# Threshold attention and two MoE layers: the last score tile of each head in one pass, its main term added inside the maximum

## The chip, the cores and the metric

One core of one Trainium2 chip. The metric is device time in microseconds (us) of one launch; lower is better. The kernel before took 969.99 us, the median of three runs (968.16 to 970.31 us).

## The reference, cut to what matters

Attention over 4 batches, 8 heads, 576 positions and 64 channels, with a threshold that is relative to each row's maximum; then two feed-forward layers over 2304 tokens. Only the attention is touched.

```python
scores = scale * np.matmul(q, k.transpose(0, 1, 3, 2))
thresh = np.max(scores, axis=-1, keepdims=True) - tau
scores = np.where(scores >= thresh, scores, -1000000000.0)
...
attn = np.exp(scores)
attn = attn / (np.sum(attn, axis=-1, keepdims=True) + 1e-09)
return np.matmul(attn, v).astype(np.float32)
```

## The kernel before, in words

**Numbers in two halves.** TensorE multiplies in a shortened fp32 (fp32r), so every operand is split into a high part and a low rest. A product is the high-by-high term (the main term) plus two cross terms. For each head, `q_st` holds q's low part on partitions 0 to 63 and its high part on 64 to 127; `k_st` holds k's high part on 0 to 63 and its low part on 64 to 127. One pass over 128 partitions therefore gives both cross terms at once. A second pass over `q_m` (q's high part on partitions 0 to 63, and rows for the shift under them) and `k_on` gives the main term.

**Attention twice over.** For each of 32 heads the kernel first computes scores with queries on partitions, only to find each query's maximum: `scores` (L319) makes five tiles of 128 queries by 576 keys, two passes of two matmuls of 288 columns each, and `row_max` (L335, its instruction L339) reduces each tile on VectorE into one column of `mcol`. 576 queries are four and a half tiles, so the fifth tile (n = 4) has 64 real queries; its other 64 stationary columns are zeros, put into `q_st[:, 576:640]` once by `setup_fill` (L181). `row_shift` (L343) turns the maxima into shifts, `shift_turn` transposes them and `shift_store` (L366) copies them with ScalarE (L369) and issues a DMA from ScalarE's own queue (L370) that puts them into `q_m`.

Then `shifted` (L390, matmuls L403) computes the scores once more with keys on partitions, less the shift, `expo` (L416) takes the exponential on ScalarE, `mask` (L421) zeroes what lies under the threshold on VectorE, `p_split` splits the result (L429 on ScalarE, L430 on GpSimd), and `values` (L435, matmuls L453) multiplies by V: three groups of two matmuls for each tile, high P by high V, high P by low V, low P by high V. `v_hi` is 128 columns wide: 64 of V, and 64 of ones, of which one gives the row sums. `v_lo` is 64 wide. `store_head` (L459) copies a finished head out of PSUM on ScalarE (`xs`, L465), and SyncE's DMA queue stores it (L467, L468).

**Order.** Heads go in pairs; a pair has nine units of work, 144 units in all, each with one tile of shifted scores. I call nine units of a pair a round. The instructions of each unit are emitted in an order written out by hand, one string for each place in the round (`ORDER`, L71): E is the shifted tile and its exponential (and, where due, the turn and store of the shifts), S a score tile, x a maximum, M the mask, v one group of value matmuls, V the rest of them, L the store of a finished head, P the transposes of a later head (L271), F its split (L279 on ScalarE, L280 on VectorE), T loads and the DMAs that stack K and Q, p the split of P. Each engine runs its own instructions in that order. The last score tile of a pair's first head falls on unit 3 of a round, that of its second head on unit 7 (15 rounds have both; the two heads of the first pair come in a ramp ahead):

```python
"FESvSSxxMxxpVLAPTJ",     # unit 3 of the round
"FEvvSvSSMxxxVLPvATpJ",   # unit 7
"FSEvPSSTMxxxpVLAJ",      # unit 8
```

**Buffers.** Scores, shifted scores and transposes share three PSUM buffers; one goes to the next tile in the order in which the tiles before were released (a score tile by its maximum, a shifted tile by its mask, a transpose by its split). The value sums have one PSUM buffer, which is free for the next head when `xs` has been copied out. In unit 7 the first head of the pair is stored; in unit 8 the value sums of the second begin.

**Stacking.** `stack_k` (L285) and `stack_q` (L293) fill the stacked operands by DMAs of the SyncE queue: `k_both` from `q_st` (L289) and from `lo` (L290), `q_m` from `q_st` (L291), and two units later `q_st` from `lo` (L295).

Of the kernel before, what the change touches and what calls it, by code (L numbers as in the profile page):

```python
# [9 lines left out]
F32 = mybir.dt.float32  # L10
# [11 lines left out]
def kernel(  # L22
# [83 lines left out]
    def f32(ap):  # L106
        return ap.bitcast(F32)
# [51 lines left out]
    q_st = bufs4([P, SP], F32R, "q_st")  # L159
    q_m = bufs4([R3, SP], F32R, "q_m")  # L160
    NV = 10
    v_nat = [early_p.tile([P, NV, D], F32, name=f"v_nat{i}") for i in range(2)]
    v_hi = [att_p.tile([P, NV, P], F32R, name=f"v_hi{i}") for i in range(2)]
    v_lo = [att_p.tile([P, NV, D], F32R, name=f"v_lo{i}") for i in range(2)]
    scale2 = const.tile([P, 1], F32, name="scale2")
    nat_both = [early_p.tile([P, 2, NM + 1, 2, D], F32, name=f"nat{i}") for i in range(2)]
# [13 lines left out]

    def setup_fill(i, eng):  # L181

        for j in range(2):
            if i < NBUF[j]:
                pad = slice(S, SP) if j == 0 else slice(0, 64)
                eng.memset(f32(k_st[j][i][:, pad]), 0.0)
                eng.memset(f32(k_on[j][i][:, pad]), 0.0)
                eng.memset(f32(k_on[j][i][D:R3, 64 * j : 64 * j + S]), 1.0)
                eng.memset(f32(k_on[j][i][D:R1, 64 * j : 64 * j + S]), 0.0)
                eng.memset(f32(q_st[j][i][:, S:SP]), 0.0)  # L190
                eng.memset(f32(q_m[j][i][0:D, S:SP]), 0.0)
                eng.memset(f32(q_m[j][i][D:R3, :]), 0.0)
# [5 lines left out]

    def setup_ones():
        for t in v_hi:  # L200
            nc.gpsimd.memset(f32(t[:, 0:8, D:P]), 1.0)
            for half in range(2):
                for n in range(2):
                    nc.gpsimd.memset(f32(t[64 * half : 64 * half + 64, 8 + n, D:P]), float(n == half))

    nat_t = {}
    k_rows, q_rows, v_rows = (a.rearrange("b h s d -> (b h s) d") for a in (k, q, v))
# [77 lines left out]
    def stack_k(h):  # L285
        j, i = buf(h)
        o = slice(key_off(h), key_off(h) + S)
        kh = f32(q_st[j][i][0:D, 0:S]).unsqueeze(1).to_broadcast([D, 2, S])
        nc.sync.dma_start(f32(k_both[j][i][0:D, :, o]), kh)  # L289
        nc.sync.dma_start(f32(k_st[j][i][D:P, o]), f32(tr_t[h][0:D, :]))  # L290
        nc.sync.dma_start(f32(q_m[j][i][0:D, 0:S]), f32(q_st[j][i][D:P, 0:S]))  # L291

    def stack_q(h):  # L293
        j, i = buf(h)
# [2 lines left out]
    def split_first():  # L297

        srcs = [tr_t[h] for h in range(2)]
        for h in range(2):  # L300
            split_kq(h)
            j, i = buf(h)
            o = slice(key_off(h), key_off(h) + S)
            nc.scalar.copy(k_st[j][i][0:D, o], f32(q_st[j][i][0:D, 0:S]))
            nc.vector.tensor_copy(k_on[j][i][0:D, o], srcs[h][0:D])
            nc.sync.dma_start(f32(k_st[j][i][D:P, o]), f32(tr_t[h][0:D, :]))
            stack_q(h)
            nc.gpsimd.tensor_copy(q_m[j][i][0:D, 0:S], f32(q_st[j][i][D:P, 0:S]))

    def keep_warm(n):  # L310

# [3 lines left out]

    sc_ps = {}
    mcol = {}

    def scores(h, n):  # L319
        j, i = buf(h)  # L320
        o = key_off(h)
        ps = ps_r.tile([P, 2, 512], F32, tag="r", name="sc")
        for st, kk in ((q_st, k_st), (q_m, k_on)):
            r = slice(0, P if st is q_st else R1)
            for c in range(2):
                nc.tensor.matmul(  # L326
                    ps[:, c, 0:HS],
                    lhsT=st[j][i][r, n * P : n * P + P],
                    rhs=kk[j][i][r, o + c * HS : o + (c + 1) * HS],
                    start=(st is q_st),  # L330
                    stop=(st is q_m),
                )
        sc_ps[h, n] = ps

    def row_max(h, n):  # L335
        if n == 0:
            mcol[h] = att_p.tile([P, NTI], F32, tag="mcol", name="mcol", bufs=2)
        mc = mcol[h]
        nc.vector.tensor_reduce(  # L339
            mc[:, n : n + 1], sc_ps.pop((h, n))[:, :, 0:HS], axis=AXES.XY, op=ALU.max, negate=True  # L340
        )
# [93 lines left out]
    def values(u, j):  # L435
# [12 lines left out]
            av_ps[h] = ps_av.tile([P, 2, 512], F32, tag="av", name="av")  # L448
        ps = av_ps[h]
        vh, vl = v_hi[p % 2][:, vn, :], v_lo[p % 2][:, vn, :]  # L450
        for o, vv, pp in ((P, vh, hi), (D, vl, hi), (P, vh, lo)):
            for c in range(2):
                nc.tensor.matmul(  # L453
                    ps[0:o, c, 0:HS], lhsT=vv, rhs=pp[:, c, :],
                    start=first and pp is hi and o == P, stop=last and pp is lo,
                )
            yield

    def store_head(h):  # L459
# [2 lines left out]
            xs = att_p.tile([P, 2, HS], F32, tag="xs", name="xs", bufs=2)  # L462
        else:
            xs = raw_p.tile([P, 1024], F32, tag="raw", name="xs")[:, 0:S].rearrange("p (c s) -> p c s", c=2)
        nc.scalar.copy(xs, av_ps.pop(h)[:, :, 0:HS])  # L465
        r = slice(D * (hh % 2), D * (hh % 2) + D)
        nc.sync.dma_start(sums_d[b][hh : hh + 1, :], xs[D : D + 1].rearrange("p c s -> p (c s)"))  # L467
        nc.sync.dma_start(x[r, hh // 2, b * S : (b + 1) * S], xs[0:D].rearrange("p c s -> p (c s)"))  # L468
# [250 lines left out]
    def attention_unit(u):  # L719
# [6 lines left out]
        av = itertools.chain(*av)  # L726
        sc = iter(s_at.get(u, ()))
        mx = iter(s_at.get(u, ()))
        for what in ORDER[u % UNITS]:
            if what == "E" and 0 <= u < NU:  # L730
                shifted(u)
# [7 lines left out]
                    scores(*a)  # L739
            elif what == "x":  # L740
                for _, a in itertools.islice(mx, 1):
                    row_max(*a)
            elif what == "M" and 0 <= u < NU:
                mask(u)
            elif what == "p" and 0 <= u - 1 < NU:
                p_split(u - 1)
            elif what == "V":
# [423 lines left out]
```

## Time and profile before

| what | value |
|---|---|
| median of three runs | 969.99 us |
| the profiled execution | 968.04 us, of which the span from first to last instruction 966.3 us |
| granted TensorE clock, mean | 0.999 |
| TensorE matmul busy | 944.8 us (98%), 5299 matmuls |
| VectorE, ScalarE, GpSimd busy | 711.9, 493.9, 603.3 us |
| attention | about the first 365 us; the two layers follow |

Busy time of TensorE is modelled, since matmuls overlap: what tells its pace is the distance from one start to the next. PEld is the weight load that goes ahead of each matmul. In a timeline row the first number is the start, the second the time taken, x2 says that two instructions are merged, and the bracket is the idle time before with what ended it.

### The profile page before, as it was taken

How to read it: one execution, taken by the hardware profiler on the slowest of the kernel's cores; microseconds unless marked ns; L12 is line 12 of the kernel's file. 1: busy time of each engine (PE TensorE's matmuls, PEld its weight loads, DVE VectorE, ACT ScalarE, POOL GpSimd, SP SyncE). 2: the span in 40 equal slices, each digit the busy share in tenths (PEclk: the TensorE clock that was granted, in tenths of full speed). 3: DMA queues.
4: the chain of work that ended last, by engine and by line, in shares of the span. 5: the costliest groups of instructions: out<-in, count | busy, mean ns of one | idle time of the engine just before them, and what ended most of it. 6: DMA issues, size and time to landing. Idle time of an engine off the chain costs nothing.

```text
span 966.3 us, 15184 instructions
## 1 busy us (share of the span) xinstructions
PE 944.8 (98%) x5299; PEld 842.3 (87%) x5299; DVE 711.9 (74%) x1132; ACT 493.9 (51%) x924; POOL 603.3 (62%) x575
## 2 busy tenths in 40 slices
PE   7999999999999989999999999999999999999998
PEld 7899899999989978889888988898889988888886
DVE  5788888788788875898678876888675676666562
ACT  3667677777767675354333433333334444344433
POOL 7678788888978898677445544654547614334422
PEclk9999999999999999999999999999999999999999
DMA  6665666657666314211311131112311124444443
GB/s 144 148 147 124 152 159 145 170 126 176 157 142 154 81 44 98 68 66 44 120 44 66 44 119 45 65 45 77 129 34 45 44 66 131 109 120 124 138 119 90
DMA packets 89726, 99.61 MB, mean 103 GB/s; under 512 B 50000, under 2 KB 62608, under 8 KB 89648
## 3 DMA queue, kind: packets, MB, share of 16 engines
q1 hardware_dynamic: 87952, 97.97, 38.5%
q8 instruction: 42, 0.69, 0.3%
q10 hardware_dynamic: 1696, 0.66, 0.3%
q14 instruction: 36, 0.29, 0.1%
HBM read 55.13 MB, written 15.88 MB: 73 GB/s over the span
## 4 chain that ended last, share of the span: by engine, by line
PE 79%; POOL 8%; issue 4%; DVE 4%; ACT 3%; DMA 1%; ACTq 0%; POOLq 0%; DVEq 0%
PE y L833 18%; PE h L793 18%; PE o L988 10%; PE h L877 10%; PE av L453 9%; PE zt L403 6%; PE sc L326 6%; POOL plo L430 3%; PE tr L271 1%; POOL wg L560 1%; DMA nat<-in_q_dram 1%; DVE mcol L339 1%; POOL dec_a L531 1%; POOL xl L769 1%; ACT phi L429 1%
## 5 line engine op out<-in xcount | busy, mean ns | idle before, releaser
L430 POOL TENSOR_TENSOR plo<-e,phi 128x576 fp32r<-128x576 f32 x144 | 207.6, 1451 | 48.9 <-ACT phi L429 48.8
L816 POOL TENSOR_TENSOR gl<-cl,gh 128x512 fp32r<-128x512 f32 (+1 forms) x80 | 100.3, 1254 | 160.0 <-ACT gh L815 85.3
L793 PE MATMUL h<-xh,wg 128*128 128x512 f32 (+1 forms) x640 | 184.1, 369 | 0.7 <-DVE e L421 0.7
L833 PE MATMUL y<-gh,wg 128*128 128x512 f32 (+1 forms) x640 | 184.6, 369 | 0.0
L421 DVE SCALAR_TENSOR_TENSOR e<-zt,ntau,e 128x576 f32<-128x576 f32 x144 | 117.3, 815 | 54.5 <-ACT e L416 34.8
L793 PEld LDWEIGHTS h<-xh,wg 128*128 128x128 f32 x640 | 118.4, 188 | 16.7 <-DVE e L421 1.0
L833 PEld LDWEIGHTS y<-gh,wg 128*128 128x128 f32 x640 | 118.5, 188 | 15.9
L416 ACT ACTIVATE e<-zt 128x576 f32<-128x576 f32 x144 | 93.9, 652 | 70.0 <-PE zt L403 53.2
L339 DVE TENSOR_REDUCE mcol<-sc 128x1 f32<-128x576 f32 x160 | 116.7, 748 | 4.9 <-PE sc L326 4.7
L833 PE MATMUL y<-gl,wg 128*128 128x512 f32 (+1 forms) x320 | 118.8, 371 | 0.9 <-POOL gl L816 0.9
L793 PE MATMUL h<-xl,wg 128*128 128x512 f32 (+1 forms) x320 | 117.8, 368 | 0.0
L815 ACT CAST gh<-cl 128x512 fp32r<-128x512 f32 (+1 forms) x80 | 46.3, 579 | 111.9 <-DVE cl L814 110.7
L812 ACT ACTIVATE cl<-cl,half 128x512 f32<-128x512 f32 (+1 forms) x80 | 54.4, 679 | 95.4 <-DVE cl L811 95.4
L988 PE MATMUL o<-wg,ln 128*128 128x512 f32 x432 | 102.7, 393 | 0.0
L877 PE MATMUL h<-wg,y 128*128 128x512 f32 x432 | 101.1, 390 | 0.0
L988 PEld LDWEIGHTS o<-wg,ln 128*128 128x128 f32 x432 | 80.9, 188 | 18.8 <-ACT ln L951 0.4
L429 ACT CAST phi<-e 128x576 fp32r<-128x576 f32 x144 | 96.2, 668 | 1.5 <-ACT mt L369 0.7
L952 POOL TENSOR_TENSOR ln<-land,ln 128x1024 fp32r<-128x1024 f32 x16 | 38.5, 2404 | 91.7 <-ACT ln L951 85.0
L877 PEld LDWEIGHTS h<-wg,y 128*128 128x128 f32 x432 | 81.0, 188 | 16.8
L811 DVE TENSOR_SCALAR cl<-h 128x512 f32<-128x512 f32 (+1 forms) x80 | 50.6, 632 | 51.1 <-PE h L793 49.0
L326 PE MATMUL sc<-k_both,q_st 128*128 128x288 f32 x320 | 72.2, 307 | 6.5 <-issue 1.8
L403 PE MATMUL zt<-q_st,k_both 128*128 128x288 f32 x320 | 72.4, 308 | 1.6 <-DVE lo L280 1.3
(114 smaller groups left out, 1883.2 us busy)
## 6 DMA issues: line engine op xcount, KB each, us to landing
raw<-in_moe_w_in_dram SPq DMA_DIRECT2D x24, 512.0 KB
raw<-in_moe_w_out_dram SPq DMA_DIRECT2D x24, 512.0 KB
k_both<-q_st SPq DMA_DIRECT2D x30, 288.0 KB
sq<-so SPq DMA_DIRECT2D x64, 128.0 KB
land<-sq SPq DMA_DIRECT2D x16, 512.0 KB
k_both<-lo SPq DMA_DIRECT2D x32, 144.0 KB
q_st<-lo SPq DMA_DIRECT2D x32, 144.0 KB
x<-xs SPq DMA_DIRECT2D x32, 144.0 KB
```

Source lines behind the costliest of these rows:

```text
L326: nc.tensor.matmul(ps[:, c, 0:HS], lhsT=st[j][i][r, n * P : n * P + P], rhs=kk[j][i][r, o + c * HS : o + (c + 1) * HS], start=(st is q_st) ...
L339: nc.vector.tensor_reduce(mc[:, n : n + 1], sc_ps.pop((h, n))[:, :, 0:HS], axis=AXES.XY, op=ALU.max, negate=True)
L403: nc.tensor.matmul(ps[:, c, 0:HS], lhsT=st, rhs=mv[:, c * HS : (c + 1) * HS], start=(m == 0), stop=(m == len(todo) - 1),)
L416: nc.scalar.activation(out=e, in_=st_ps[u][:, :, 0:HS], func=ACTF.Exp)
L421: nc.vector.scalar_tensor_tensor(out=e, in0=st_ps.pop(u)[:, :, 0:HS], scalar=ntau[:, 0:1], in1=e, op0=ALU.is_ge, op1=ALU.mult)
L429: nc.scalar.copy(hi, e)
L430: (nc.vector if u - NU in LO_DVE or u < NU - UNITS and u % UNITS in LO_UNITS else nc.gpsimd).tensor_tensor(lo, e, f32(hi), op=ALU.subtract)
L793: nc.tensor.matmul(ps, lhsT=a[:, kk, f], rhs=m[:, kk, :], start=(n == 0 and kk == 0), stop=(n == 2 and kk == KD - 1),)
L816: nc.gpsimd.tensor_tensor(gl, cl, f32(gh), op=ALU.subtract)
L833: nc.tensor.matmul(y_ps[c][d], lhsT=a[:, jj, ds_], rhs=m, start=(jj == 0 and n == 0), stop=(jj == JG - 1 and n == 2),)
L877: nc.tensor.matmul(ps[g], lhsT=a[:, kk, :], rhs=wg_t["in2", g][s][:, kk, :], start=(n < 2), stop=(n >= 6 * KD - 2),)
L988: nc.tensor.matmul(ps, lhsT=a[:, f, :], rhs=wg_t["out2", f // 4][m][:, f % 4, :], start=(n == 0), stop=(n == len(terms) - 1))
```

## The change

In `scores`, the fifth tile does only the first pass. For that, the zero columns of `q_st` (partitions 0 to 63) get q's high part of the last 64 queries, by one more DMA in `stack_k` (by GpSimd for the first two heads); the stationary's other 64 columns then give the main term on PSUM partitions 64 to 127 in the same pass. In `row_max`, the fifth tile is copied from those partitions to an SBUF tile `main` of 64 x 576 by ScalarE, and a `tensor_tensor_reduce` on VectorE adds it to the cross terms and takes the maximum; that operation comes behind the mask of its unit. `mcol` becomes two fixed tiles, zeroed once. `v_hi` becomes 66 columns wide, and `xs` copies 65 partitions.

```diff
+    VW = D + 2
-    v_hi = [att_p.tile([P, NV, P], F32R, name=f"v_hi{i}") for i in range(2)]
+    v_hi = [att_p.tile([P, NV, VW], F32R, name=f"v_hi{i}") for i in range(2)]
...
     def setup_fill(i, eng):
+        if i < 2:
+            eng.memset(mcols[i], 0.0)
...
-            nc.gpsimd.memset(f32(t[:, 0:8, D:P]), 1.0)
+            nc.gpsimd.memset(f32(t[:, 0:8, D:VW]), 1.0)
...
         nc.sync.dma_start(f32(q_m[j][i][0:D, 0:S]), f32(q_st[j][i][D:P, 0:S]))
+        nc.sync.dma_start(f32(q_st[j][i][0:D, S:SP]), f32(q_st[j][i][D:P, M4:S]))
...
             nc.gpsimd.tensor_copy(q_m[j][i][0:D, 0:S], f32(q_st[j][i][D:P, 0:S]))
+            nc.gpsimd.tensor_copy(q_st[j][i][0:D, S:SP], f32(q_st[j][i][D:P, M4:S]))
...
+    mcols = [att_p.tile([P, NTI], F32, name=f"mcol{i}") for i in range(2)]
...
-        for st, kk in ((q_st, k_st), (q_m, k_on)):
+        passes = ((q_st, k_st), (q_m, k_on))[0 : 2 if n < NM else 1]
+        for st, kk in passes:
...
-                    stop=(st is q_m),
+                    stop=(st is passes[-1][0]),
...
-            mcol[h] = att_p.tile([P, NTI], F32, tag="mcol", name="mcol", bufs=2)
+            mcol[h] = mcols[h % 2]
         mc = mcol[h]
+        if n == NM:
+            ps = sc_ps.pop((h, n))
+            t = att_p.tile([64, 2, HS], F32, tag="half", name="main", bufs=1)
+            nc.scalar.copy(t, ps[64:P, :, 0:HS])
+            def finish():
+                nc.vector.tensor_tensor_reduce(
+                    out=t, in0=ps[0:64, :, 0:HS], in1=t, scale=-1.0, scalar=3.0e38,
+                    op0=ALU.add, op1=ALU.min, accum_out=mc[0:64, n : n + 1],
+                )
+            return finish
...
-        for o, vv, pp in ((P, vh, hi), (D, vl, hi), (P, vh, lo)):
+        for o, vv, pp in ((VW, vh, hi), (D, vl, hi), (VW, vh, lo)):
...
-        nc.scalar.copy(xs, av_ps.pop(h)[:, :, 0:HS])
+        nc.scalar.copy(xs[0:R1], av_ps.pop(h)[0:R1, :, 0:HS])
...
             elif what == "x":
                 for _, a in itertools.islice(mx, 1):
-                    row_max(*a)
+                    behind.append(row_max(*a))
+                if masked:
+                    run_behind()
-            elif what == "M" and 0 <= u < NU:
-                mask(u)
+            elif what == "M":
+                if 0 <= u < NU:
+                    mask(u)
+                masked = True
+                run_behind()
```

`run_behind` calls what is in `behind`, in order; for tiles other than the fifth, `row_max` has emitted its instruction at once and there is nothing to call.

## Rows read from the trace of the kernel before

**Rows 1.** Busy time of each engine in two stretches (PE, PEld, DVE, ACT, POOL).
```profile
145.00:190.00 45.00, 43.84 (x322) 41.99 (x322) 36.73 (x51) 32.42 (x63) 39.80 (x42) 1.00 0.66 162
325.00:370.00 45.00, 41.20 (x264) 36.47 (x262) 31.32 (x36) 30.72 (x58) 41.54 (x34) 1.00 0.19 45
```

**Rows 2.** Timeline of TensorE, four groups in a row, 150.8 to 152 us.
```profile
150.86 0.43 PE L453 MATMUL av<-phi,v_hi 128*128 128x288 f32 x2
151.12 0.42 PE L453 MATMUL av<-phi,v_lo 128*64 128x288 f32 x2
151.38 0.43 PE L453 MATMUL av<-plo,v_hi 128*128 128x288 f32 x2
151.65 0.42 PE L403 MATMUL zt<-q_st,k_both 128*128 128x288 f32 x2
```

**Rows 3.** Timeline, a second head's last tile (units 7 and 8), 317 to 320 us.
```profile
317.15 0.43 PE L326 MATMUL sc<-k_both,q_m 65*128 65x288 f32 x2
...
317.36 0.62 ACTq L370 DMA_DIRECT2D q_m<-mt  x1
...
317.42 0.82 DVE L421 SCALAR_TENSOR_TENSOR e<-zt,ntau,e 128x576 f32<-128x576 f32 x1 [0.35 <-ACT mt L369]
...
318.10 0.64 ACT L465 COPY xs<-av 128x576 f32<-128x576 f32 x1 [0.77 <-PE av L453]
318.16 0.75 DVE L339 TENSOR_REDUCE mcol<-sc 128x1 f32<-128x576 f32 x1
318.29 0.30 PEld L403 LDWEIGHTS zt<-q_st,k_both 128*128 128x128 f32 x2 [0.15 <-DVE e L421]
...
318.64 0.68 ACT L429 CAST phi<-e 128x576 fp32r<-128x576 f32 x1
...
318.92 0.43 PE L453 MATMUL av<-phi,v_hi 128*128 128x288 f32 x2
...
319.20 0.71 PE L271 MATMUL tr<-ident,nat 128*128 128x128 f32 x5
319.21 0.66 ACT L416 ACTIVATE e<-zt 128x576 f32<-128x576 f32 x1
```

**Rows 4.** The last round of this kind, without a later score tile, 338.9 to 340 us.
```profile
338.95 0.64 ACT L465 COPY xs<-av 128x576 f32<-128x576 f32 x1 [0.77 <-PE av L453]
...
339.64 0.53 PE L453 MATMUL av<-phi,v_hi 128*128 128x288 f32 x2 [0.42 <-ACT xs L465]
```

**Rows 5.** Line 905 (second layer): the read behind an operation with an accumulator output.
```profile
L905 DVE DVE_READ_ACCUMULATOR so<-h,st,so x36: 81/83/86, 768.2 to 944.8; 128x1 f32 x36
```

**Rows 6.** The same place in an early round, 63.9 us.
```profile
63.86 0.30 PEld L403 LDWEIGHTS zt<-q_st,k_both 128*128 128x128 f32 x2 [0.15 <-DVE e L421]
```

**Rows 7.** Timeline of TensorE around 175.6 us.
```profile
175.56 0.53 PE L453 MATMUL av<-plo,v_hi 128*128 128x288 f32 x2 [0.15 <-POOL plo L430]
```

**Rows 8.** Timeline after a first head's last tile (units 3 and 4), 201 to 205 us.
```profile
201.66 0.55 SPq L295 DMA_DIRECT2D q_st<-lo  x1
...
203.14 0.42 PE L403 MATMUL zt<-q_st,k_both 128*128 128x288 f32 x2
...
204.18 0.30 PEld L326 LDWEIGHTS sc<-k_both,q_st 128*128 128x128 f32 x2
```

**Rows 9.** Line 326, 202.5 to 205.5 us: TensorE's semaphore waits (min/median/max ns, starts).
```profile
L326 PEldq EVENT_SEMAPHORE  x2: 51/574/1096, 202.9 to 203.1; - x2
```

**Rows 10.** SyncE's DMA queue, 196 to 199 us: one issue of stack_k.
```profile
197.13 0.60 SPq L291 DMA_DIRECT2D q_m<-q_st  x1
```

**Rows 11.** What SyncE's queue waits for, 100 to 370 us (total, times, longest).
```profile
SPq L467 <- ACT xs L465: 58.4, 16, 10.6
```

**Rows 12.** GpSimd, the first 30 us: the ones of v_hi.
```profile
L201 POOL MEMSET v_hi<- 128x512 f32 x2 | 1.1, 526 | 0.1
```

**Rows 13.** Groups by line and shape, 100 to 370 us.
```profile
L453 PEld LDWEIGHTS av<-phi,v_hi 128*128 128x128 f32 x254 | 40.3, 189 | 2.6 <-ACT xs L465 1.7
...
L453 PEld LDWEIGHTS av<-phi,v_lo 128*64 128x64 f32 x256 | 33.9, 135 | 0.0
```

More of the change, by code (lines that the diff above doesn't have):

```diff
@@ L200, in setup_ones @@
         for t in v_hi:
-            nc.gpsimd.memset(f32(t[:, 0:8, D:P]), 1.0)
+            nc.gpsimd.memset(f32(t[:, 0:8, D:VW]), 1.0)
             for half in range(2):
                 for n in range(2):
-                    nc.gpsimd.memset(f32(t[64 * half : 64 * half + 64, 8 + n, D:P]), float(n == half))
+                    nc.gpsimd.memset(f32(t[64 * half : 64 * half + 64, 8 + n, D:VW]), float(n == half))
     nat_t = {}
@@ L454, in values @@
                     ps[0:o, c, 0:HS], lhsT=vv, rhs=pp[:, c, :],
-                    start=first and pp is hi and o == P, stop=last and pp is lo,
+                    start=first and pp is hi and o == VW, stop=last and pp is lo,
                 )
@@ L728, in attention_unit, with run_behind @@
         mx = iter(s_at.get(u, ()))
+        masked, behind = False, []
+        def run_behind():
+            while behind:
+                f = behind.pop(0)
+                if f:
+                    f()
         for what in ORDER[u % UNITS]:
```

## The prediction

> **What bounds the kernel now.** The change lies in the attention, so I read that stretch first, by busy time per engine: TensorE is busy 43.8 of 45 us, VectorE 36.7, GpSimd 39.8, ScalarE 32.4 [rows 1]. The groups by line come next, for durations; then the timeline of TensorE, because its busy time is modelled and only the distance of starts tells its pace: two matmuls of 288 columns take 0.26 us, 0.132 each [rows 2]. In the whole stretch there are 322 in 45 us, 0.140 each [rows 1]. So TensorE sets the pace, and of a round, nine units with 152 matmuls, only some 1.2 us are waits. The reader must see where these waits stand, for time saved just ahead of a wait is not saved. Hence the timelines of the two places that the change touches, unit by unit.
>
> **What is removed.** 32 heads lose two matmuls each: 64 x 0.132 = 8.4 us, 0.26 us a head. That is the whole prize, if nothing waits behind it.
>
> **Second heads (unit 7), 15 rounds.** ScalarE issues a DMA from 317.36 to 317.98 [rows 3]; `xs` follows at 318.10 to 318.74, `phi` 0.10 before its end, `e` at 319.21. The value sums need `xs` to have left their buffer, the transposes need the score tile's buffer. TensorE starts the values at 318.92 and the transposes at 319.20 [rows 3]. Step by step after the change:
>
> The score tile ends 0.26 us earlier, and the next one starts earlier. But the shifted tile behind them waits already now: its weight load stands 0.15 us for the mask, which ends at 318.24 [rows 3]. The mask is not moved, so the 0.26 us becomes more of that wait. Gain: nothing.
>
> The copy to `main` is emitted behind the DMA issue and ahead of `xs`. The trace has no copy from 64 partitions of PSUM; the nearest is `xs` itself, 0.64 us, with the same columns [rows 3]. If time went with partitions it would be 0.32 (an estimate); I take 0.64. So `main` takes 318.10 to 318.74, `xs` 318.64 to 319.28, and `phi` and `e` come 0.54 later. The values then start 0.05 after `xs` ends, as in the round where they wait for it now (338.95 + 0.64, then 339.64 [rows 4]): 319.33 instead of 318.92, 0.41 later. A pair of matmuls after a wait takes 0.53 instead of 0.43 [rows 3, 4], another 0.10: transposes at 319.70.
>
> They wait for VectorE as well. The new reduction reads PSUM and SBUF like the mask, 0.82 us [rows 3], and has an accumulator to read, 0.08 [rows 5]: 0.90. It starts some 0.08 after `main` ends (as the mask after its copy) and ends at 319.72; transposes at 319.77, 0.57 later than now. No row shows this operation. Bounds: 0.75, a plain maximum [rows 3], and 1.57 if it made an elementwise pass (0.82) and a maximum (0.75) one after the other; I take 0.90, its two parts having rows. Price of a regular round: 0.50 to 0.57, say 0.55. ScalarE, late by 0.54 too, has no gap until the split of the transposes, so what follows moves as a whole and nothing is won back.
>
> Seven of the 15 rounds look like this to the hundredth (the first and the last of them: [rows 3, 6]): 7 x 0.55 = 3.9. In four, the score tile of unit 8 already starts up to 0.25 later for another reason, and part of the wait is there: 4 x 0.45 = 1.8. In two, TensorE later waits 0.4 us for a GpSimd that works without a gap, 0.15 and a slow restart in one row [rows 7], the same at 260 us; that swallows the delay: 0.1 each. One waits a full microsecond for a transfer just before, and the last runs into the tail where GpSimd is busy 41.5 of 45 us [rows 1]: 0.1 each. Sum: **+6.0 us**.
>
> **First heads (unit 3), 15 rounds.** Here `main` falls between `e` and `phi`, and the reduction behind the mask. TensorE begins the next shifted tile at 203.14, and could some 0.2 earlier. Then it stops: the first load of the next score tile stands at 204.18 [rows 8], and the sequencer had waited 1.10 us, from 203.1 on, until then [rows 9]. What comes last there is the transfer `q_st<-lo`, issued at 201.66 [rows 8]; its queue hangs on `xs` of unit 2, which the change does not touch. So the gain is swallowed. In the few rounds where the transfer is early about 0.1 is left: **-0.4 us** in all. At worst none, at best 15 x 0.26 = 3.9. The two heads of the ramp come where TensorE waits for transfers: nothing. `phi` moves by 0.54 ahead of GpSimd, which has room in unit 3.
>
> **The rest.** VectorE works 0.15 us longer a head, beside the waits above. One more DMA a head: an issue takes 0.60 us of SyncE's queue [rows 10], which waits 58 us for `xs` in this stretch [rows 11]; the tile that needs it comes units later. Taken as nothing; with its cover gone up to 0.6 in the two rounds where a score tile waits for a transfer, +1.2. The set-up fills 1.05 us less of ones [rows 12], and adds two small fills and two copies: between -1.0 and +0.5 (an estimate), taken as nothing, since heads wait there for transfers. `xs` with 65 partitions: nothing, at best 0.3 a head, if time went with partitions.
>
> Narrower `v_hi`: its load takes 189 ns, the 64-column load of `v_lo` 135 [rows 13], yet the groups with `v_lo` keep the same 0.26 us as the others [rows 2]. The load is hidden under the matmul before: nothing. By the Trainium skill ("TensorE: Matmul & The Clock Gate", section "LDWEIGHTS (loading the stationary operand)"), a load's time goes with its columns, 0.83 ns each, so 62 fewer would save an estimated 52 ns on each of 640 loads, 33 us, if loads set the pace; that rule agrees with the two durations, not with the pace.
>
> **Sum.** +6.0 - 0.4 = +5.6 us. The profiled execution took 968.04, so 973.6 by its own time; the median shown is 1.95 above it, and against that I predict **975.6 us**. What a measurement can tell from no change is about 0.2%, 1.9 us.
>
> **Rivals.**
> 1. *The saved passes arrive.* All 8.4 us, if the waits in units 7 and 3 move with them: 961.6. For it: TensorE is the busiest engine. Against it: the mask, `xs` and the transfer end when they did, or later [rows 3, 8]. Chance 0.11.
> 2. *It cancels.* The first heads keep most of their 0.26 (-3), the second heads lose only half, because later waits for GpSimd and transfers take up delay [rows 7] (+3.5): 970 to 971. For it: every round has such waits. Chance 0.17.
> 3. *The reduction is slow.* At 1.57 us it ends at 320.47 [rows 3, 5], and the transposes come 1.3 us late instead of 0.55; it decides from about 0.9 us on. Thirteen rounds more by 0.75: 985. No row excludes it; that the mask reads the same two sources in one pass [rows 3] speaks against it. Chance 0.08.
> 4. *Weight loads set the pace.* 640 x (189 - 135) ns = 34 us less [rows 13]: 936. Against it: the pace [rows 2]. Chance 0.04. By the rule of the Trainium skill above it would be the outcome.
>
> That the fifth tile keeps two passes can't be: the text of `scores` gives it one.
>
> **The numbers.** My forecast has 0.60, with 973 to 978 as its own range. Slower by over 0.2%: 0.60 and rival 3, 0.68. Rivals 1 and 4 and a quarter of rival 2 are faster: 0.19. The rest of rival 2 is the same: 0.13. The range leaves out rivals 3 and 4 and the farther half of rival 1, and takes in the bounds of the DMA, the fills and the first heads: 962 to 981.
>
> **What would show it.** In the profile after: line 326 with 64 matmuls fewer; in unit 7 `main` directly behind the DMA issue and `xs` half a microsecond later; TensorE's waits for `xs` in some ten rounds, where there are now few; the shifted tile of unit 8 waiting 0.4 instead of 0.15; the score tile of unit 4 still starting with the transfer; the pace of the value groups still 0.26. I am wrong if TensorE starts the values of unit 8 no later than now after the shifted tile of unit 7, if rounds become shorter, or if the reduction takes over a microsecond.

## The result, and the profile after

The changed kernel takes **984.86 us**, median of six runs (981.34 to 986.41); the kernel before, median of six, 970.15 (968.16 to 974.18). The ratio is 1.014, with an interval from 1.0111 to 1.0169. I had predicted 975.6, with a range of 962 to 981: the direction was right, but the loss is 14.7 us where I had 5.6. The profiled execution took 986.41 us with a span of 984.6, which is 18.3 above the span before. One launch of an experiment below (one pass for first heads, no decoding) took 1575.11 us at a mean granted clock of 0.554, and its ratio leaves that launch out.

The busy times by stage of the changed kernel, the same two stretches and columns as in [rows 1]:

```profile
145.00:190.00 45.00, 43.08 (x303) 39.27 (x302) 37.30 (x53) 34.24 (x67) 37.89 (x38) 1.00 0.63 152
325.00:370.00 45.00, 40.19 (x274) 37.20 (x275) 32.16 (x44) 31.20 (x61) 37.40 (x38) 0.96 0.32 79
```

In 45 us TensorE starts 303 matmuls where it started 322: part of that is the two passes gone from each round; TensorE is still the busiest engine, and it waits more. The groups by line and shape, 100 to 370 us, answer to [rows 13] (count, then busy us and mean ns, then idle time before and who ended it):

```profile
L472 PEld LDWEIGHTS av<-phi,v_hi 128*66 128x66 f32 x246 | 31.9, 138 | 8.5 <-ACT xs L484 7.4
...
L352 DVE CUSTOM_DVE_ANT_0 main<-sc,main 64x576 f32<-64x576 f32 x24 | 17.9, 744 | 5.4 <-ACT main L349 5.4
L349 ACT COPY main<-sc 64x576 f32<-64x576 f32 x24 | 15.3, 637 | 8.6 <-PE av L472 8.4
L484 ACT COPY xs<-av 65x576 f32<-65x576 f32 x24 | 15.3, 636 | 9.5 <-PE av L472 7.7 <-DMA k_both<-q_st 0.8 <-DMA raw<-in_moe_w_out_dram 0.8
```

Three prices that the trace before could not give: the copy to `main` takes 637 ns, the fused addition and maximum 744 ns, and `xs` with 65 partitions 636 ns, as with 128. TensorE's wait for `xs` has grown from 1.7 us [rows 13] to 7.4.

**Where the time went.** I set the start of every unit's shifted tile in the two traces side by side and add up how much longer each unit of the round is, over the 14 full rounds behind the ramp (units 9 to 134; a unit of the table is its place in the round, 0 to 8):

| part | profiled run of after less before, us |
|---|---|
| up to the start of unit 0 (the ramp) | +4.1 |
| round 0 | +0.5 |
| units 3, 4, 5 (first heads): -2.5, +8.2, +2.0 | +7.7 |
| units 6, 7, 8, 0, 1, 2 (second heads): 0, -1.6, +7.9, +0.6, -0.7, 0 | +6.1 |
| last round and the two layers | -0.1 |

The second heads cost what was predicted (+6.0). The first heads were to win 0.4 and lose 7.7, and the ramp was to cost nothing.

**Second heads.** The timeline of units 7 and 8 in the changed kernel, to be laid beside [rows 3]:

```profile
244.30 0.62 ACTq L389 DMA_DIRECT2D q_m<-mt  x1
244.39 0.80 DVE L440 SCALAR_TENSOR_TENSOR e<-zt,ntau,e 128x576 f32<-128x576 f32 x1
...
244.96 0.64 ACT L349 COPY main<-sc 64x576 f32<-64x576 f32 x1 [0.69 <-PE av L472]
245.25 0.53 PE L422 MATMUL zt<-q_st,k_both 128*128 128x288 f32 x2
...
245.62 0.64 ACT L484 COPY xs<-av 65x576 f32<-65x576 f32 x1
245.63 0.75 DVE L352 CUSTOM_DVE_ANT_0 main<-sc,main 64x576 f32<-64x576 f32 x1 [0.44 <-ACT main L349]
246.16 0.67 ACT L448 CAST phi<-e 128x576 fp32r<-128x576 f32 x1
246.31 0.48 PE L472 MATMUL av<-phi,v_hi 128*66 128x288 f32 x2 [0.27 <-ACT xs L484]
246.31 0.07 DVE L352 DVE_READ_ACCUMULATOR2_ANT mcol<- 64x1 f32 x1
...
246.63 0.71 PE L274 MATMUL tr<-ident,nat 128*128 128x128 f32 x5
```

`main` stands directly behind the DMA issue, `xs` behind `main`, and the values start 0.05 us after `xs` ends (245.62 + 0.64, then 246.31). The reduction and its read [rows 5] end together at 246.38, so the reduction takes 0.75 in all, not 0.90, and the transposes follow TensorE's own order. The shifted tile waits for the mask, which ends at 245.19. Of the prediction's steps at this place, the wait for the mask and the wait for `xs` are there; the reduction ends too early to matter.

**First heads.** Unit 4 of the same round, from its shifted tile to that of unit 5. Before:

```profile
139.32 0.42 PE L403 MATMUL zt<-q_st,k_both 128*128 128x288 f32 x2
139.43 1.43 POOL L430 TENSOR_TENSOR plo<-e,phi 128x576 fp32r<-128x576 f32 x1 [0.35 <-ACT phi L429]
...
139.64 0.81 DVE L421 SCALAR_TENSOR_TENSOR e<-zt,ntau,e 128x576 f32<-128x576 f32 x1
...
140.36 1.04 DVE L520 SCALAR_TENSOR_TENSOR dec_a<-raw,dec_a 128x512 uint32<-128x512 uint32 x1
...
141.34 0.82 DVE L421 SCALAR_TENSOR_TENSOR e<-zt,ntau,e 128x576 f32<-128x576 f32 x1
...
142.43 0.43 PE L403 MATMUL zt<-q_st,k_both 128*128 128x288 f32 x2
```

And after:

```profile
146.26 0.64 ACT L349 COPY main<-sc 64x576 f32<-64x576 f32 x1
146.45 0.81 DVE L440 SCALAR_TENSOR_TENSOR e<-zt,ntau,e 128x576 f32<-128x576 f32 x1
...
146.58 0.53 PE L422 MATMUL zt<-q_st,k_both 128*128 128x288 f32 x2
146.80 0.67 ACT L448 CAST phi<-e 128x576 fp32r<-128x576 f32 x1
...
147.17 0.74 DVE L352 CUSTOM_DVE_ANT_0 main<-sc,main 64x576 f32<-64x576 f32 x1
...
147.55 1.60 POOL L449 TENSOR_TENSOR plo<-e,phi 128x576 fp32r<-128x576 f32 x1 [1.00 <-ACT phi L448]
...
147.84 1.86 DVE L539 SCALAR_TENSOR_TENSOR dec_a<-raw,dec_a 128x512 uint32<-128x512 uint32 x1
...
149.63 0.80 DVE L440 SCALAR_TENSOR_TENSOR e<-zt,ntau,e 128x576 f32<-128x576 f32 x1
...
150.48 0.30 PEld L422 LDWEIGHTS zt<-q_st,k_both 128*128 128x128 f32 x2 [0.80 <-DVE e L440]
```

The reader is to follow three rows. `main` pushes `phi`, so GpSimd's `plo` runs to 149.15, which is 2.57 us after the start of unit 4 (before: 1.54). Between the masks VectorE makes a step of the decoding of the layers' weights (L539, before L520), an operation that reads two SBUF tiles. It takes 1.86 us now, 1.04 before, and it ends 0.55 and 0.54 after `plo` (149.70 against 149.15; 141.40 against 140.86). With no split beside it, it takes 0.68, as in an early round of the kernel before:

```profile
55.73 0.68 DVE L520 SCALAR_TENSOR_TENSOR dec_a<-raw,dec_a 128x512 uint32<-128x512 uint32 x1
```

It holds beyond this round. In both profiles, each such step of unit 4 that starts inside a split (13 of 15 before, 15 of 15 after) ends 0.54 to 0.56 us after the split, and has then taken between 0.68 and 1.89 us. The mask stands behind the step in VectorE's order, and the shifted tile of unit 5 waits 0.8 us for that mask.

**The ramp.** Busy times and TensorE's granted clock by stage (columns as in [rows 1]). Before, from 14 to 16 us:

```profile
14.00:16.00 2.00, 2.00 (x18) 2.00 (x17) 2.00 (x4) 0.00 (x0) 1.82 (x5) 1.00 0.96 239
```

After, from 12 us on:

```profile
12.00:14.00 2.00, 0.35 (x1) 0.38 (x2) 0.36 (x1) 0.00 (x0) 1.77 (x7) 0.83 1.08 290
14.00:16.00 2.00, 2.00 (x11) 1.97 (x10) 1.22 (x2) 0.00 (x0) 1.83 (x5) 0.50 0.84 171
...
18.00:20.00 2.00, 2.00 (x10) 1.97 (x10) 0.98 (x3) 0.64 (x1) 0.00 (x0) 0.50 0.51 115
```

After a stretch in which it had almost nothing to do, TensorE runs from 14 to 20 us at a granted clock of 0.50, the 1.2 GHz level, with 10 or 11 matmuls in 2 us instead of 18. What it had waited for is the first score tile's operand. The timeline of the changed kernel:

```profile
9.56 0.44 ACTq L252 DMA_DIRECT2D v_nat<-in_v_dram  x1
...
13.65 0.82 PE L333 MATMUL sc<-k_both,q_st 128*128 128x288 f32 x2 [3.05 <-DMA q_st<-lo]
```

and that of the kernel before:

```profile
9.80 0.42 ACTq L249 DMA_DIRECT2D v_nat<-in_v_dram  x1
...
12.27 0.50 PE L326 MATMUL sc<-k_both,q_st 128*128 128x288 f32 x2 [1.42 <-DMA q_st<-lo]
```

The transfers that stack the first heads were issued at the same times (the second `q_st<-lo` at 10.85 and 10.89), but ScalarE's load of V a quarter of a microsecond sooner. The clock fell once more, to 0.73 between 325 and 330 us. In the run with V loaded by SyncE (below) it stayed at 1.00 there, and units 4 and 5 add 2.3 us less over all rounds; so some 2 us of the first heads' 7.7 go with the clock.

### The profile page after: what moved, and what is told of

Its sections match the earlier page's. It is cut to its first block, busy times and chain, and to the rows that moved or that the text cites. A ratio compares the mean times of both kernels' runs of the same rounds, so it can differ in the third digit from the quotient of the medians.

```text
span 984.6 us, 15184 instructions
## 1 busy us (share of the span) xinstructions
PE 950.8 (97%) x5235; PEld 835.0 (85%) x5235; DVE 725.0 (74%) x1164; ACT 514.0 (52%) x956; POOL 603.2 (61%) x579
## 4 chain that ended last, share of the span: by engine, by line
PE 51%; DVE 17%; ACT 9%; issue 8%; POOL 8%; DMA 5%; ACTq 1%; SPq 1%; POOLq 0%; DVEq 0%
PE h L825 17%; PE y L865 17%; PE av L472 5%; PE zt L422 4%; PE sc L333 3%; POOL plo L449 2%; DVE so L937 2%; DVE e L440 2%; DVE so L964 2%; ACT phi L448 2%; PE o L1020 2%; DVE st L925 2%; DVE so L949 2%; ACT xs L484 1%; ACT so L929 1%
## 5 line engine op out<-in xcount | busy, mean ns | idle before, releaser
L449 POOL TENSOR_TENSOR plo<-e,phi 128x576 fp32r<-128x576 f32 x144 | 210.8, 1471 | 63.1 <-ACT phi L448 60.4
L358 DVE TENSOR_REDUCE mcol<-sc 128x1 f32<-128x576 f32 x128 | 93.1, 747 | 3.5 <-PE sc L333 3.4
L333 PE MATMUL sc<-k_both,q_st 128*128 128x288 f32 x320 | 74.7, 316 | 9.0 <-DMA q_st<-lo 5.6
L422 PE MATMUL zt<-q_st,k_both 128*128 128x288 f32 x320 | 75.2, 316 | 6.6 <-DVE e L440 4.4
```

The lines of the kernel that those rows point to most:

```text
L333: nc.tensor.matmul(ps[:, c, 0:HS], lhsT=st[j][i][r, n * P : n * P + P], rhs=kk[j][i][r, o + c * HS : o + (c + 1) * HS], start=(st is q_st) ...
L358: nc.vector.tensor_reduce(mc[:, n : n + 1], sc_ps.pop((h, n))[:, :, 0:HS], axis=AXES.XY, op=ALU.max, negate=True)
L422: nc.tensor.matmul(ps[:, c, 0:HS], lhsT=st, rhs=mv[:, c * HS : (c + 1) * HS], start=(m == 0), stop=(m == len(todo) - 1),)
L449: (nc.vector if u - NU in LO_DVE or u < NU - UNITS and u % UNITS in LO_UNITS else nc.gpsimd).tensor_tensor(lo, e, f32(hi), op=ALU.subtract)
```

## The experiments

Theory after the result: two separate costs, one for each kind of head (waits behind `xs` in unit 8; the collision of `plo` with the decoding step in unit 4), and a ramp that is late for its transfers. Rivals: narrower operands, the added DMA, a slow reduction, or a disturbance that has nothing to do with the change. "Unit 135" is the start of the last round, where all full rounds lie behind. Unless another partner is named, the comparison is with the kernel before.

**One pass for first heads alone.**

```diff
-        passes = ((q_st, k_st), (q_m, k_on))[0 : 2 if n < NM else 1]
+        passes = ((q_st, k_st), (q_m, k_on))[0 : 1 if n == NM and h % 2 == 0 else 2]
...
-        if n == NM:
+        if n == NM and h % 2 == 0:
```

> The one-pass tile for the first head of each pair only; the second head's last tile has its two passes and its plain maximum again. Theory (the loss has two seats: ScalarE's extra copy ahead of xs in units 7 and 8 costs 6 us; in units 3 to 5 the copy delays phi, GpSimd's subtraction then runs over VectorE's weight-decoding operation and holds it, and the next mask and tile come 0.7 us late): about 6 us below the changed kernel, still 5 to 8 us above the kernel before; unit 8 as before, unit 4 still longer by 0.7 to 0.9 us. Rival (the added DMAs and the set-up cost most of it): hardly below the changed kernel, both units still long.

975.06 us, ratio 1.007 (1.0052 to 1.0088). Unit 3 is 0.23 shorter in the median round, unit 4 0.81 longer, unit 8 unchanged; units 3 to 5 add up to +5.7 and unit 135 comes 5.8 later. The first heads alone lose what I had expected of the second.

**One pass for second heads alone** (the same two lines with `h % 2 == 1`).

> The one-pass tile for the second head of each pair only. Theory: units 3 to 5 as before, with the decoding operation at about 1.0 us again instead of 1.85; unit 8 longer by 0.5 to 0.6 us in most rounds; about 6 us above the kernel before, plus up to 4 us where TensorE's clock falls in the ramp. Rival (added DMAs): unit 4 stays long, 12 us or more above.

976.67 us, 1.0086 (1.007 to 1.0102). Unit 8 is 0.47 to 0.61 longer in 8 of 14 rounds (median 0.49), unit 3 unchanged, the median unit 4 longer by 0.03; unit 135 comes 7.5 later. With the run before: two costs, which add up to 13.3 at unit 135, where the changed kernel has 14.3 behind its ramp.

**The split of P ahead of the copy in unit 3.**

```diff
-        "FESvSSxxMxxpVLAPTJ",
+        "FESvSSMpxxxxVLAPTJ",
```

> The changed kernel, but in unit 3 the split of P (phi, then GpSimd's plo) is emitted ahead of the new copy and not behind it. Same work, one place in the order. Theory: plo starts 2.2 us into unit 3 again (2.87 in the changed kernel), VectorE's decoding operation takes about 1.0 us instead of 1.85, the mask of unit 4 and the tile of unit 5 come 0.7 us earlier in about ten rounds: 6 to 8 us below the changed kernel. Rival (the transfer q_st<-lo has become later through the added DMA and sets the start of unit 4's score tile): no change in unit 4, within 1 us of the changed kernel.

980.04 us, 1.0114 (1.0088 to 1.0141). Against the kernel before, each beside its own runs, that is 11.2 more, and the changed kernel had 14.7 more. The gain is smaller than the 6 to 8 us expected, and the two intervals overlap, so the time alone doesn't show it. The traces do: units 3 to 5 add 3.9 us instead of 7.7. Unit 4 of the round shown above:

```profile
147.34 1.42 POOL L449 TENSOR_TENSOR plo<-e,phi 128x576 fp32r<-128x576 f32 x1 [0.33 <-ACT phi L448]
...
147.96 0.75 DVE L352 CUSTOM_DVE_ANT_0 main<-sc,main 64x576 f32<-64x576 f32 x1 [0.24 <-ACT main L349]
148.64 0.68 DVE L539 SCALAR_TENSOR_TENSOR dec_a<-raw,dec_a 128x512 uint32<-128x512 uint32 x1
...
149.24 0.80 DVE L440 SCALAR_TENSOR_TENSOR e<-zt,ntau,e 128x576 f32<-128x576 f32 x1
```

The split has 0.12 us left when the decoding step starts, and the step takes 0.68 us instead of 1.86. The median unit 4 is longer than in the kernel before by 0.24 instead of 0.83. So the collision is shown, but not that the first heads then win.

**Narrow `v_hi` and `xs` alone**, in the kernel before.

```diff
+    VW = D + 2
-    v_hi = [att_p.tile([P, NV, P], F32R, name=f"v_hi{i}") for i in range(2)]
+    v_hi = [att_p.tile([P, NV, VW], F32R, name=f"v_hi{i}") for i in range(2)]
...
-        nc.scalar.copy(xs, av_ps.pop(h)[:, :, 0:HS])
+        nc.scalar.copy(xs[0:R1], av_ps.pop(h)[0:R1, :, 0:HS])
```

> The kernel before with v_hi 66 columns wide instead of 128 and xs of 65 partitions; nothing else of the change. Theory (a weight load is hidden under the matmul before it): the pace of the value groups stays 0.26 us, the time is that of the kernel before within 2 us. Rival (loads set the pace): 30 us less.

969.38 us, 1.0002 (0.9985 to 1.0019): nothing. Its timeline, beside [rows 2]:

```profile
151.22 0.43 PE L454 MATMUL av<-phi,v_lo 128*64 128x288 f32 x2
151.49 0.43 PE L454 MATMUL av<-plo,v_hi 128*66 128x288 f32 x2
```

The loads are shorter (138 ns for 189) and the pairs of matmuls start 0.26 us apart as before.

**The added transfers and set-up alone** (two passes and the plain maximum for every tile; the rest of the change stays).

```diff
-        passes = ((q_st, k_st), (q_m, k_on))[0 : 2 if n < NM else 1]
+        passes = ((q_st, k_st), (q_m, k_on))
...
-        if n == NM:
+        if n > NM:
```

> The changed kernel with two passes and the plain maximum for every tile: what is left of the change is the added DMA a head, the fills, the fixed mcol and the narrow v_hi. Theory (none of these costs anything): within 2 us of the kernel before, unit 4 and unit 8 as before. Rival (the added DMA makes q_st<-lo later, so unit 4's score tile starts later): 4 us or more above it.

969.85 us against 967.78, 1.0021 (1.001 to 1.0032); unit 135 comes 1.3 later, from units 4 and 7 of single rounds (0.82, 0.42, 0.37, 0.56 the largest), while most rounds don't change. That is the pattern of a score tile that now and then waits for its operand: in this run TensorE's score matmuls waited 1.7 us for `q_st<-lo` between 45 and 360 us. One to two microseconds in all, which I had taken as nothing. That they are the DMA's is likely, not shown: the run has the set-up and the narrow operands too, and in the profiled run of these alone, which has no added DMA, unit 135 came 1.5 later as well, mostly by one unit 4 (1.80).

**Second heads alone, with the copy behind `xs`.**

```diff
-        "FEvvSvSSMxxxVLPvATpJ",
+        "FEvvSvSSMVLxxxPvATpJ",
```

> The one-pass tile for second heads only (as in e2, 976.7 us), but in unit 7 the copy to main is emitted behind xs and not ahead of it. xs then ends when it did in the kernel before, and main 0.54 later than in e2, the reduction behind it. Theory (two waits stand at that place, for xs and, a little later, for the score tile's buffer): the values of unit 8 start on time, but the transposes wait for the reduction, some 1.0 us later than in the kernel before: 5 to 8 us above e2. Rival (xs alone is what costs): the 7 to 8 us of e2 vanish, about 969 us.

984.18 us, 1.0169 (1.0156 to 1.0183); unit 8 is now 1.19 longer in the median round. Unit 8 in the timeline:

```profile
288.09 0.64 ACT L484 COPY xs<-av 65x576 f32<-65x576 f32 x1 [0.75 <-PE av L472]
288.75 0.64 ACT L349 COPY main<-sc 64x576 f32<-64x576 f32 x1
...
289.42 0.75 DVE L352 CUSTOM_DVE_ANT_0 main<-sc,main 64x576 f32<-64x576 f32 x1 [1.17 <-ACT main L349]
...
290.23 0.53 PEld L274 LDWEIGHTS tr<-ident,nat 128*128 128x128 f32 x5 [0.55 <-DVE mcol L352]
```

`xs` is early, but the score tile's buffer now comes late: the transposes wait for the reduction. Two waits stand there: the copy put ahead of `xs` makes `xs` late, and put behind it makes the reduction late.

**The kernel before, with the transfers of unit 2 issued earlier.** The traces had shown unit 4 waiting for a transfer of stacking in some rounds.

```diff
-        "EvvSvSSMxxxVLFPATpJ",
+        "EvvSvSSMxxxTVLFPApJ",
```

> The kernel before, but in unit 2 the DMAs of T (q_st<-lo among them) are emitted ahead of the store of the finished head and not behind it, so that q_st<-lo no longer waits in SyncE's queue for xs. Theory (that transfer sets the start of unit 4's score tile in most rounds): q_st<-lo is issued about 2 us earlier, TensorE's waits at that tile (0.05 to 1.8 us a round) vanish, 2 to 5 us below the kernel before. Rival (the tile waits for something else): no change.

**965.79 us**, 0.9975 (0.9964 to 0.9986): faster than both kernels. Unit 4 is shorter in four rounds by 0.54, 0.90, 1.62 and 0.56, and in the other ten by 0.2 at most. So the transfer set its start in four rounds of 14, not in most, as the theory and the prediction had it.

**First heads alone, with both orders** (the split ahead of the copy, the transfers early).

> The one-pass tile for first heads only (e1, 975.1 us), with phi ahead of the copy in unit 3 (as in e3) and the DMAs of T ahead of the store in unit 2 (as in e7). Theory (the two things that swallowed this gain are then both gone): unit 3 shorter by 0.2 us and unit 4 not longer, 6 to 9 us below e1, that is 2 us or more below e7 less its own gain. Rival (the one-pass tile of first heads costs something else): at or above the kernel before.

968.62 us, 1.0012 (1.0002 to 1.0022), that is 2.8 above the run before. The gain on the first heads alone is there (6.4), the 2 us below the run before are not. A miss: unit 3 keeps its gain (-0.22), but unit 4 is 0.24 longer in nearly every round, with no collision and no late transfer in the way. The timeline shows why:

```profile
139.78 0.75 DVE L352 CUSTOM_DVE_ANT_0 main<-sc,main 64x576 f32<-64x576 f32 x1 [0.25 <-ACT main L349]
...
140.47 0.07 DVE L352 DVE_READ_ACCUMULATOR2_ANT mcol<- 64x1 f32 x1
140.59 0.30 PEld L333 LDWEIGHTS sc<-k_both,q_st 128*128 128x128 f32 x2
```

The second score tile of unit 4 needs the buffer that the reduction reads. With the split ahead, the copy and the reduction are later; their end, 140.54, lets the tile's load start at 140.59. That is not the whole 0.24. Some 0.1 stands at the start of the unit: its shifted tile, now earlier, waits 0.19 us for the split of the transposes on VectorE (L283), and after that wait its first pair of matmuls takes 0.37 us to the next instead of 0.27.

**The first load of V three units later**, in the changed kernel.

```diff
-    at(late_, -6, load_v, 0, nc.scalar)
+    at(late_, -3, load_v, 0, nc.scalar)
```

> The changed kernel, with the first load of V issued three units later, so that it no longer shares the transfers' time with the stacking of the first head. In the changed kernel's profile the first score tile started at 13.65 us (before: 12.27), TensorE had been idle for 3 us until then, and the granted clock was 0.50 from 14 to 20 us; unit 0 began 4.1 us later. Theory (the ramp's loss comes from the stacking transfers landing behind that load): the first score tile starts at 12.0 to 12.6 us, the clock stays near 1.0 up to 22 us, unit 0 begins at 20 to 21 us; 980 to 982 us, 3 to 4 less than the changed kernel. Rival (the low clock comes by chance with the longer idle time of every ramp, or the stack is late for another reason): the first score tile still at 13 us or later, 984 to 985.

984.22 us (982.99 to 987.54), as the changed kernel. Half of the theory held: the first score tile started at 11.90 us and the clock was full to 18 us. But ScalarE's three issues of the load, 16.80 to 18.81, now stood ahead of the first shifts; TensorE was busy 0.48 of the 2 us up to 20, the clock was 0.50 from 20 to 26 us, and unit 0 began at 23.01.

**No decoding within the attention.** To see the first heads without the operation that collides, the next three leave no decoding step in the attention's units and do it all at its end; the transfers of unit 2 are early in all three.

```diff
-    JOBS_FROM = 1
+    JOBS_FROM = 200
...
+            jobs.finish()
             moe1_in(0, IN_EARLY.index(u - NU))
```

The partner, with two passes for all:

> The kernel before, with the transfers of unit 2 issued early (as in the version that beat both), and with all decoding of the weights of the layers taken out of the attention's units and put at its end. Same results, much longer after the attention; only its attention is read, as the partner of the next run. VectorE then has only the mask between units 3 and 4. Expected: the mask of unit 4 ends with the exponential, about 4.8 us after the start of unit 3; the total 20 to 150 us above the kernel before, from the decoding at the end.

One pass for first heads:

> One pass for the first heads only, copy ahead of the split as in the changed kernel, transfers of unit 2 early, no decoding within the attention: to be compared with the run before it. Theory (the first heads' saving is lost because VectorE's decoding operation runs into GpSimd's split and holds the mask of unit 4): with no decoding there, unit 3 is shorter by 0.2 us a round and unit 4 no longer than in the partner, so that unit 135 begins 2 to 3 us earlier than in the partner (ramp aside), and the total is 1 to 3 us less. Rival (something else takes it back: the transfer, GpSimd, ScalarE later by 0.54): unit 4 or 5 longer by 0.2 or more a round, unit 135 and the total the same as the partner's or later.

The same with the split ahead of the copy:

> As the run before, with the split of P put ahead of the copy in unit 3, so that GpSimd is not late either. Theory: as the run before, 2 to 3 us earlier than the partner at unit 135; no difference from the run before of more than 1 us, since the order of copy and split matters only by the decoding that the split runs into. Rival (GpSimd's lateness itself costs): the run before loses its saving and this one has it, 2 us or more apart.

1003.34, 1001.61 and 1002.59 us (the decoding at the end makes all three long; ratios to the kernel before 1.0359, 1.0341 and 1.035, each within 0.0025). Against the partner, the first heads now **win**: unit 3 is 0.21 shorter, unit 4 0.09 longer, and the way from unit 0 to unit 135 is 1.9 us shorter; the total is 1.7 less. `plo` is as late as in the changed kernel, and the mask of unit 4 no longer minds:

```profile
136.11 0.74 DVE L352 CUSTOM_DVE_ANT_0 main<-sc,main 64x576 f32<-64x576 f32 x1
...
136.51 1.42 POOL L449 TENSOR_TENSOR plo<-e,phi 128x576 fp32r<-128x576 f32 x1 [1.03 <-ACT phi L448]
...
137.63 0.82 DVE L440 SCALAR_TENSOR_TENSOR e<-zt,ntau,e 128x576 f32<-128x576 f32 x1 [0.77 <-ACT e L435]
...
138.55 0.35 PE L422 MATMUL zt<-q_st,k_both 128*128 128x288 f32 x1
```

The 0.09 is the slow start of the shifted tile that the run with both orders showed. With the split ahead unit 4 is again 0.24 longer, of which some 0.15 is left for the buffer, so the order of the two matters even without decoding. I had expected a microsecond at most between the two: it is 1.0. From unit 0 to unit 135 I had expected a gain of 2 to 3 us in both; it is 1.9 and, with the split ahead, 0.9.

**The load of V issued by SyncE**, behind the stacking, in the changed kernel.

```diff
-    at(late_, -6, load_v, 0, nc.scalar)
+    at(late_, -6, load_v, 0, nc.sync)
```

> The changed kernel, with the first load of V issued by SyncE's queue behind the stacking transfers instead of by ScalarE among them. Theory (the load, issued just ahead of the second head's stacking, makes the transfers of the stack late, and nothing else lengthens the ramp): first score tile at 11.9 to 12.6 us, no idle stretch of TensorE over 1.5 us after it, granted clock 1.0 from 12 to 26 us, unit 0 at 20 to 21 us, median 980 to 982, and the runs within 2 us of each other. Rival 1 (the load only moves the loss, as in the run with the load three units later: V comes too late and the first values wait): unit 0 or unit 1 late by 2 us or more, 983 to 986. Rival 2 (the clock is low by chance, whatever the transfers do): first score tile early and the clock at the lower level all the same.

**980.52 us** (980.37 to 982.49), 1.0139 (1.0124 to 1.0155). The first score tile starts at 12.09, the clock is 1.00 from 12 to 26 us, unit 0 begins at 20.55 (before: 20.41), and the runs lie within 2.2 us of each other. So the ramp up to unit 0 is undisturbed; in round 0 the clock falls all the same, to 0.50 from 28 to 30 us, after 2 us in which TensorE was busy for 0.84. The table above, for this run: ramp and round 0 +0.8, units 3 to 5 +5.7, the others +6.0. Unit 135 comes 12.5 later, the span is 12.4 longer. By the medians the gain over the changed kernel is small: 12.8 us above the kernel before beside it (967.71), against 14.7, and the two ratios' intervals overlap.

**All three remedies together** (V by SyncE, the split ahead in unit 3, the transfers of unit 2 early).

> The changed kernel with the three remedies together: V's first load by SyncE, in unit 3 the split of P ahead of the copy, the transfers of unit 2 issued early. Theory (what is left of the loss is the second heads' two waits, about 6 to 8 us, on the version of before with early transfers, 965.8): 972 to 975 us, unit 4 within 0.2 of the early version's, unit 8 longer by 0.5 to 0.6 in nearly every round. Rival (the parts of the loss depend on each other, so that removing some brings out others): 977 or more.

975.27 us, 1.0077 (1.0065 to 1.009), just above what I expected. Against the version with early transfers units 6 to 2 add 6.7 us (6.0 above); units 3 to 5 still add 1.7 (the median unit 4 is 0.23 longer, and two rounds lose 0.75 and 1.80 there); ramp and round 0 add 1.8. No form of the change with the decoding in its place beats the version of before with the same remedy.

## Why the prediction was right and wrong

- **What bounds.** Right: TensorE sets the pace and the waits decide. In no run did the removed 8.4 us arrive; the best case, first heads without decoding, got 1.9 of the 3.9 that their 15 rounds had to give.
- **Second heads, +6.0.** Right in mechanism and size: 6.0 in the run with an undisturbed ramp, with `xs` 0.66 behind `main` and unit 8 longer by 0.5. Even the exceptions came as forecast: in the two rounds in which a wait for GpSimd was to swallow the delay (one is [rows 7]) unit 1 is 0.42 shorter, and in the round with a microsecond's wait ahead unit 7 is 1.0 shorter. One term was off without consequence: the reduction takes 0.75 with its read (0.90 taken), so it ends in time, and `xs` alone sets the price. Why second heads alone were 7.5 late, and not 6.0, is not shown.
- **First heads, -0.4: the step that failed.** I wrote "`phi` moves by 0.54 ahead of GpSimd, which has room in unit 3", took that as costing nothing, and had the gain swallowed by the transfer. GpSimd had room, but VectorE had not: the split that moved into its next operation made that operation 0.8 us longer, and the mask behind it was the next thing that TensorE needed. Measured: +5.7 with an undisturbed ramp. The split ahead of the copy takes the lengthening away, and without decoding the first heads win 1.9, so this cause is shown. I had asked what waits for `phi`, not what runs beside `plo`. The rule was there to be read: the Trainium skill ("SBUF — State Buffer", section "Who interferes with whom") says that a VectorE instruction with two SBUF inputs contends with a GpSimd instruction that reads SBUF, since the ports they share are held by one of them alone. The rows agree: the decoding step ends 0.55 us after `plo` and takes 0.68 when nothing runs beside it. And a mask, which has one source in PSUM, takes its 0.81 in the middle of a `plo` (139.64, above). The size stood in the trace before: its steps of unit 4 took 1.03 us with 0.48 of the split left, 1.35 with 0.80 and 1.55 with 1.00.
- **The transfer that swallows the gain.** Half right. It bound unit 4 in four rounds of 14 (early transfers give 0.25% to the kernel before); the prediction shows it in one round, [rows 8], and has it for nearly all. Beside it stand three more gates: the collision, the split of the transposes that frees the shifted tile's buffer, and, with the split of P ahead, the buffer that the reduction frees.
- **The rest.** Narrow `v_hi`: nothing, as predicted; the rival that loads set the pace is dead. The rule of the Trainium skill ("TensorE: Matmul & The Clock Gate", section "LDWEIGHTS (loading the stationary operand)") holds for the price of a column: 62 columns fewer made the load 51 ns shorter (138 for 189), 0.82 each. It does not give a load's whole time (an estimated 55 ns for 66 columns by the page's formula, 138 measured), and it speaks of the load, not of the pace; so rival 4 does not follow from it, though the prediction says so. The DMA with the set-up: 1 to 2 us instead of nothing, near the bound of 1.2 that I had kept.
- **The ramp, 0.** A term that I had put at nothing, and wrong by 4.1 us in the profiled run. Four of the six runs (984.83 to 986.41) lie 3 to 5 us above the other two (981.34 and 981.77), but only one has a trace. With V's load moved out of the way the ramp and round 0 add 0.8, so the load's place among the stacking transfers is the likely cause; that rests on few profiles. In the thirteen profiles in which ScalarE issued it there (before, after, and all experiments but three), the first score tile started at 13.65 and 13.79 us in the two where the issue came at 9.56 and 9.62, and at 11.96 to 12.54 in the eleven where it came at 9.76 or later. Why it came early, and whether it did so in the runs without a trace, is open. The mean clock only hints at it: of the changed kernel's six runs four had 0.996 or less, of 59 of the kernel before that were run beside the experiments, six; but so had two of the five with all three remedies, where SyncE issues the load.
- **Rivals.** "The reduction is slow" gave 985, where the time landed, but it isn't the cause: 0.75 us, not 1.57. "It cancels" had the right doubt, that the first heads' waits are not one wait, and the wrong sign.

Sum, by the run with an undisturbed ramp: 0.8 + 5.7 + 6.0 = 12.5, where 5.6 was predicted. The profiled run has 5.9 more, 4 in the ramp and some 2 from the lower clock behind it.

## What to carry to other kernels

When an edit delays an operation, look up what will run beside it at its new time, on every engine, not only who waits for it: here a split that was late for nobody made VectorE's next operation 0.8 us longer in most rounds. A saving of 0.26 us ahead of several gates is worth what the last of them lets through, so name the second and the third gate before the first is removed. And where two queues feed the same start, fix their order by hand: in two of thirteen profiles a load was issued a few tenths of a microsecond sooner, and the attention began 3 to 4 us later.

## What the runs showed of the hardware that was not expected

- A decoding step on VectorE (two SBUF sources, 128 x 512 words) takes 0.68 us alone, 1.04 when it starts 0.50 before the end of GpSimd's split and 1.86 when it starts 1.31 before; each time it ends 0.55 after the split. The split that began first is sometimes longer as well (1.60 us at 147.55, but 1.43 at 139.43); what lengthens it is open.
- The fused addition and maximum with one source in PSUM takes 744 ns for 64 x 576, as long as the plain maximum over 128 partitions (746 ns), and is not disturbed by a split that runs beside it (147.17 and 147.55 above).
- A PSUM copy on ScalarE takes 0.64 us for 64, 65 or 128 partitions alike.
- After 3 us almost without matmuls TensorE worked 6 us at the 1.2 GHz level although it was busy without a gap (14 to 20 us). In the run with the late load it did so again, from 20 to 26 us, after 2 us in which it was busy for 0.48. In the kernel before it was busy for 0.81 from 26 to 28 us, and the clock stayed at 1.00.
